# Zero stores of an output: some late in the filter stages, the others during the feed-forward

## The chip, the cores and the metric

One core of one Trainium2 chip runs the whole program. The metric is the device time of one execution in microseconds; lower is better. Before the change three runs took 1114.2 us (median), between 1113.84 and 1117.29.

## The reference, cut to what matters

```
X = rfft(x, axis=1); Y = X * (filt_r + i filt_i); x = irfft(Y)      # x: 8 batches, 3072 rows, 256 columns
x = x.reshape(24576, 256)
logits = x @ w_gate; expert = argmax(logits); gate = max softmax of the logits
for i in order: if counts[expert[i]] < 768: the row gets the next slot of its expert
y = relu(slots @ w1) @ w2                                            # 8 experts, 768 slots each
out = zeros(24576, 256); out[i] = gate[i] * y[slot of i] where i has a slot
out = elu(out @ w_in) @ w_out                                        # 256 -> 2048 -> 256
```

Only 6144 of the 24576 rows have a slot. A row without one is zero before the last product and so stays zero behind it: the output is 24 MB of zeros with 6144 rows written over them.

## The kernel before, in words

The program has two parts. The **filter stages** take the batches one by one. Three batches are taken at first (`run(3, True, "f")`); if these fill every expert, which a flag tells at the end, nothing else is done, and else all is done again with eight batches. In the profiled run the three are enough. Per batch `b` there are three generators: `p1` transforms over n1 in 8 steps of 4 rows (L195 and after), `p2` does the transform over n2, the filter and the transform back over k2 in 17 steps, and `p3` goes back to tokens in 18 steps and queues their rows for the slots. `route(b)` finds the slots, in small steps on VectorE. The loop of `run` weaves them: `p2(b)`, then the rest of `p1(b + 1)` with steps of `route(b)`, then `p3(b)` with the rest of `route(b)` and, in its last three steps, the first three of `p2(b + 1)`. The order of instructions on each engine is the order in which this Python code calls them (`manual_schedule`); engines wait for each other by semaphores.

GpSimd stores the rows to their slots in DRAM with indirect DMAs (`scatter`, L363), drawn from the queue `pq` by `pool_tick`. The second queue, `dq`, holds the **zero stores**: `zero_out(n)` writes the 1024 rows n of the output (1 MB) from a tile of zeros, with one DMA issued on ScalarE's queue (L432). `dma_tick` takes one from `dq`. Before the change `dq` gets all 24 behind the first `p1`, and is ticked on even steps below 12 of `p2(b)` for b > 0, on steps 4 to 7 of `p1(b + 1)`, and on every fourth step of `p3(b)` but for the last batch. Since the last three steps of `p3` take three of `p2`, the loop over `p2(1)` and `p2(2)` sees steps 3 to 16 and ticks at 4, 6, 8 and 10. That makes 4 + 5 + 4 + 4 + 5 ticks up to the end of `p3(1)`, and the last two stores go at steps 4 and 6 of `p2(2)`.

SP issues all loads: the rows of x (L187), the experts' weights (L516 and L520, `fetch`, called by `more_raw`), the rows of a chunk of slots (L538). Late in `p2(2)` it loads the first expert's weights; `load_piece` splits them (ScalarE's cast `wp`, L529, and a subtraction).

The **feed-forward** takes 16 chunks of 384 slots. `e1` does an expert's two products on a chunk (`ph` and `py`, in 8 blocks of hidden units), `e2` the shared two (`ph2`, then `po`, in 16 blocks). `do_e2` runs five chunks behind `do_e1`. In `e2` a block is six products into PSUM (three buffers), two activations on ScalarE (L632, L633), one operation on VectorE that reads PSUM for the last time (L634), a cast and a subtraction for the split in two parts, and six products into `po`, which run three blocks late. Behind the last block three indirect DMAs on GpSimd write 384 rows to their places in the output (L666). They wait for the zero stores before them, since both write the output; among themselves they are declared free of order (group `g_out`).

Of the kernel before, what the change touches and what calls it, by code (L numbers as in the profile page):

```python
# [25 lines left out]

# columns of the packed constant table
C_ID, C_WA, C_WD, C_TRI, C_ONE, C_KEY, C_RST, C_TOK = 0, 128, 224, 320, 416, 512, 520, 776
# [3 lines left out]
def shape_tables():  # L32
    """Transform matrices and index tables; they depend on the shapes alone.

    s = 32 n1 + n2 and f = k1 + 96 k2: a transform over n1, one over n2 per unit k1 = 1..47 with
    the twiddle in it, and unit 0 for the two real rows k1 = 0 and k1 = 48. The frequencies above
    S / 2 are kept as the conjugates of those below.
    """
    wa, wd = np.zeros((N1, 96)), np.zeros((96, N1))
# [52 lines left out]
class Moe:  # L92
# [23 lines left out]

    # ---------------------------------------------------------------- constants
    def consts(self, pool):
# [29 lines left out]
    def warm_up(self):  # L148
        """Keeps the tensor engine's clock up until the first rows are there."""
        ps = self.ps.tile([128, 128], F32, tag="pl", name="pwarm")  # L150
        z = self.zero[:, :128]
        for _ in range(10):
            self.nc.tensor.matmul(ps, lhsT=z, rhs=z, start=True, stop=True)

    # ---------------------------------------------------------------- filter tables
    def load_filters(self, g):
        """A third of the filter's rows and of the transforms over n2 and k2."""
        nc = self.nc
        big = self.big
        if g == 0:  # L160
            self.frt, self.fit, self.wbt, self.wct = [], [], [], []
        wb = big.tile([128, 8, 128], F32, tag="B", name="wbt", bufs=NBUF)
        nc.sync.dma_start(wb, self.wb[:, 8 * g : 8 * g + 8])
        for i in range(2):
            js = slice(8 * g + 4 * i, 8 * g + 4 * i + 4)
            fi = big.tile([128, 4, D], F32, tag="B", name="fit", bufs=NBUF)
            nc.sync.dma_start(fi[0:64], self.fi[0:64, js])
            fr = big.tile([128, 4, D], F32, tag="B", name="frt", bufs=NBUF)
            nc.sync.dma_start(fr, self.fr[:, js])
            self.fit.append(fi)  # L170
            self.frt.append(fr)
        wc = big.tile([128, 8, 128], F32, tag="B", name="wct", bufs=NBUF)
        nc.sync.dma_start(wc, self.wc[:, 8 * g : 8 * g + 8])
        self.wbt.append(wb)
        self.wct.append(wc)
# [6 lines left out]

    # ---------------------------------------------------------------- spectral filter of a batch
    def load_x(self, b, t):
# [9 lines left out]
    def p1(self, b):  # L194
        """The transform over n1: zt[d, m, n2]."""  # L195
        nc = self.nc
        self.zt = [self.big.tile([128, 96, N2], F32, tag="Z", name="zt", bufs=2) for h in range(2)]
        for t in range(8):
            xt = self.xq.popleft()
            for h in range(2):  # L200
                ps = self.ps.tile([128, 4, 96], F32, tag="pa" if h else "pb", name="pz")
                for i in range(4):
                    nc.tensor.matmul(ps[:, i], lhsT=xt[:, i, h * 128 : h * 128 + 128], rhs=self.wa, start=True, stop=True)  # L203
                dst = self.zt[h][:, :, 4 * t : 4 * t + 4]
                src = ps.rearrange("p n m -> p m n")
                if h:
                    nc.vector.tensor_copy(dst, src)
                else:
                    nc.scalar.copy(dst, src)
            if b:  # L210
                self.more_x()
            yield t

    def p2(self, b):
        """Per four rows m: the transform over n2, the filter, and the transform over k2."""
        nc = self.nc
# [55 lines left out]
    def route(self, b):  # L272
        """Logits, gates and slots of a batch's tokens, in steps that yield."""
        nc = self.nc
# [76 lines left out]
        if b >= self.spec_b:  # L351
            # The first chunks are read before this batch's rows are stored: it leaves them alone.
            low = late.tile([N1, N2], F32, name="low")
            nc.vector.tensor_scalar(low, pos, float(CH), BIG, op0=ALU.is_le, op1=ALU.mult)
            nc.vector.tensor_tensor(km, km, low, op=ALU.add)
# [20 lines left out]
    def store(self, b, t, y, rt):  # L376
        """Queues the four rows a partition has in y for their slots."""
        dst, gid = rt
# [9 lines left out]
    def p3(self, b):  # L388
        """Back over m to tokens, and their rows to the slots."""
        nc = self.nc  # L390
# [37 lines left out]

    # ---------------------------------------------------------------- slots and output
    def zero_out(self, n):  # L430
        o = self.out[n * 1024 : n * 1024 + 1024].rearrange("(p r) d -> p r d", p=128)
        self.nc.scalar.dma_start(o, self.zero.unsqueeze(1).to_broadcast([128, 8, D]))  # L432

    def prefill(self):
        """Every slot starts as a row of zeros with a token out of bounds."""
        nc = self.nc
# [6 lines left out]

    # ---------------------------------------------------------------- shared weights
    def slot(self, dtype, name):
# [7 lines left out]
    def convert(self):  # L453
        """Takes the shared weights, float64 words, into two float32r parts each, in steps that yield.

        P = sign 2^(e - 31); the high part takes the first 12 bits of the mantissa, the low part
        is rounded from the 20 bits after them.
        """
        nc = self.nc
# [48 lines left out]

    # ---------------------------------------------------------------- experts' weights
    def fetch(self, e, g):  # L510
        """Loads the weights of two of an expert's blocks of hidden units."""
        nc = self.nc
# [10 lines left out]
    def load_piece(self, first=False):  # L523
        """Splits the weights of the next block of hidden units in two parts."""
        nc = self.nc
# [6 lines left out]

    # ---------------------------------------------------------------- feed-forward
    def load_rows(self, c):
# [9 lines left out]
    def prep_x(self, c):  # L544
        """A chunk's rows times their gates, turned and split, in steps that yield."""
        nc = self.nc
# [32 lines left out]
    def e1(self, c, pieces, xh, xl):  # L579
        """An expert's two products on a chunk, per block of hidden units."""  # L580
        nc = self.nc
# [36 lines left out]
    def e2(self, yt, ids, tags, eng):  # L618
        """The shared products on a chunk, per block of hidden units, and its rows out."""
        nc = self.nc  # L620
# [26 lines left out]
        def down(f, rows=range(3)):  # L647
# [4 lines left out]
            for t in rows:  # L652
# [9 lines left out]
                if f == 15:  # L662
# [7 lines left out]
                        in_offset=None,  # L670
                        bounds_check=NB * S - 1,
                        oob_is_err=False,
# [21 lines left out]
    def ffn(self):  # L694
# [50 lines left out]
        def do_e2(c, nxt):  # L745
# [4 lines left out]
            for f in range(16):  # L750
                up(f)
                flush(3)
                lag.append(lambda *rows, f=f: down(f, *rows))
                next(conv, 0)
                if nxt < n and f in (5, 8, 11):
                    if f == 5:
                        prep = self.prep_x(nxt)
                    next(prep, 0)
                    if f == 11:
                        more_rows()  # L760
# [12 lines left out]

    # ---------------------------------------------------------------- the whole
    def run(self, nb, spec, tagname):
# [5 lines left out]
        with ExitStack() as st:  # L781
# [22 lines left out]
            self.prefill()  # L804
            self.dq.extend((lambda n=n: self.zero_out(n)) for n in range(24))
            p2 = self.p2(0)
            self.ffn_open()
            for b in range(nb):
# [3 lines left out]
                for s in p2:  # L812
                    self.pool_tick()
                    if b and s % 2 == 0 and s < 12:
                        self.dma_tick()
# [9 lines left out]
                for t in p1:  # L825
                    next(rt, 0)
                    self.pool_tick(2)
                    if t > 3:
                        self.dma_tick()
# [14 lines left out]
                for s in p3:  # L844
# [4 lines left out]
                    self.pool_tick()  # L849
                    if s % 4 == 0 and not last:  # L850
                        self.dma_tick()
# [18 lines left out]
            for _ in prep:  # L870
                pass
            self.dma_tick(99)
            self.pool_tick(99)
            while len(self.pieces.get(0, [])) < 8:
# [18 lines left out]
def tile_fftconv_moe_elu(ctx, tc, x, fr, fi, wg, w1, w2, w_in, w_out, tab, wb, wc, disp, out, cap):  # L893
    k = Moe(tc, x, fr, fi, wg, w1, w2, w_in, w_out, tab, wb, wc, disp, out, cap)
    nc = tc.nc
    with tc.manual_schedule():
        if cap != 2 * CH:
            k.run(NB, False, "g")
            return
        # Three batches fill every expert, or else all of it is done again with all batches.  # L900
        flag = ctx.enter_context(tc.tile_pool(name="flag", bufs=1))
# [47 lines left out]
```

## Time and profile before

| | us |
|---|---|
| median of 3 runs | 1114.2 |
| lowest, highest | 1113.84, 1117.29 |
| profiled execution, span from its first to its last instruction | 1174.5 |
| TensorE busy in that span | 1067.7 |
| VectorE, ScalarE, GpSimd busy | 655.6, 670.5, 259.6 |

The page gives no other time for the profiled execution than its span; it is 60 us over the median of the runs without a profile. The page's rows by slices of the span show TensorE nearly always busy from about 450 us on and less before; the DMA engines are busy nearly all of the first 100 us, half until 250 us and little later.

### The profile page before, as it was taken

To read this page: it belongs to the slowest core of one execution; us is meant where nothing else is said; L and a number is where in the kernel's file an instruction comes from. 1 tells how busy PE (TensorE), PEld (TensorE's weight loads), DVE (VectorE), ACT (ScalarE), POOL (GpSimd) and SP (SyncE) were. 2 spreads that over 40 slices of the span, in tenths; PEclk is the share of its full clock that TensorE was granted. 3 is DMA by queue.
4 is the path that set the end of the run, shared out by engine and by line. 5 is a ranking of instruction groups with operands and counts; after the bars stand their busy time and mean duration, and the time that the engine had idled before them with its cause. 6 is when DMAs were issued, how large, how long until landed. Compare 5 with 4: busy or idle time off the path is not lost.

```text
span 1174.5 us, 17246 instructions
## 1 busy us (share of the span) xinstructions
PE 1067.7 (91%) x6164; PEld 982.3 (84%) x6164; DVE 655.6 (56%) x1222; ACT 670.5 (57%) x1411; POOL 259.6 (22%) x271
## 2 busy tenths in 40 slices
PE   7968789686298999999999999999999999999996
PEld 7857666564287888999999999999999999999996
DVE  1825645485169898754564455456555544555553
ACT  2625335365055547674675657467675746666664
POOL 0301570485626455400010010001101000111110
PEclk8978898798599999999999999999999999999998
DMA  9999558532245341300120030012211000000000
GB/s 251 267 211 320 177 171 275 175 102 68 69 142 169 97 146 54 91 23 14 33 68 28 1 99 15 15 32 68 63 55 33 1 15 1 14 15 14 15 15 16
DMA packets 86383, 100.89 MB, mean 86 GB/s; under 512 B 7404, under 2 KB 72385, under 8 KB 86288
## 3 DMA queue, kind: packets, MB, share of 16 engines
q1 hardware_dynamic: 54416, 61.88, 19.3%
q10 hardware_dynamic: 24960, 25.17, 6.4%
q0 software_dynamic: 6912, 12.65, 3.3%
q8 instruction: 50, 0.82, 0.3%
q14 instruction: 45, 0.37, 0.1%
HBM read 55.52 MB, written 47.31 MB: 88 GB/s over the span
## 4 chain that ended last, share of the span: by engine, by line
PE 70%; DVE 12%; issue 7%; DMA 4%; ACT 2%; POOL 2%; ACTq 1%; another core or an unknown queue 1%; SPq 0%; POOLq 0%; DVEq 0%
PE po L654 13%; PE ph L575 10%; PE ph L576 10%; PE ph L577 10%; PE po L661 7%; PE pz L203 3%; PE py L575 3%; PE py L577 3%; PE py L576 3%; DMA xt<-in_x_dram 2%; PE pv L399 2%; DVE hl L597 1%; PE pd L410 1%; PE pd L412 1%; DMA fit<-in_fi_dram 1%
## 5 line engine op out<-in xcount | busy, mean ns | idle before, releaser
L634 DVE SCALAR_TENSOR_TENSOR g<-g,ph 128x384 f32<-128x384 f32 x256 | 141.6, 553 | 237.5 <-ACT g L633 231.7
L654 PE MATMUL po<-wz,gh 128*128 128x512 f32 x576 | 210.2, 395 | 0.0
L632 ACT ACTIVATE g<-ph 128x384 f32<-128x384 f32 x256 | 125.5, 490 | 128.8 <-PE ph L577 128.3
L666 POOL DMA_INDIRECT out_dram<-o,ids x48 | 48.3, 1006 | 636.0 <-DVE o L665 625.0
L575 PE MATMUL ph<-y,wih 128*128 128x384 f32 x512 | 175.8, 343 | 1.7 <-DVE hl L597 1.0
L576 PE MATMUL ph<-y,wih 128*128 128x384 f32 x512 | 173.4, 339 | 0.0
L577 PE MATMUL ph<-y,wil 128*128 128x384 f32 x512 | 172.8, 338 | 0.0
L661 PE MATMUL po<-wz,gl 128*128 128x256 f32 x576 | 161.3, 280 | 0.0
L633 ACT ACTIVATE g<-g 128x384 f32<-128x384 f32 x256 | 134.6, 526 | 8.1
L644 DVE TENSOR_TENSOR gl<-g,gh 128x384 fp32r<-128x384 f32 x240 | 132.3, 551 | 3.7 <-ACT gh L643 3.7
L643 ACT CAST gh<-g 128x384 fp32r<-128x384 f32 x256 | 127.5, 498 | 5.2 <-PE po L654 4.0
L654 PEld LDWEIGHTS po<-wz,gh 128*128 128x128 f32 x576 | 108.1, 188 | 16.7
L597 DVE SCALAR_TENSOR_TENSOR hl<-ph,hh 128x384 fp32r<-128x384 f32 x128 | 71.0, 555 | 83.9 <-ACT hh L596 82.6
L596 ACT ACTIVATE hh<-ph 128x384 fp32r<-128x384 f32 x128 | 62.0, 489 | 87.6 <-PE ph L577 71.7
L661 PEld LDWEIGHTS po<-wz,gl 128*128 128x128 f32 x576 | 108.6, 189 | 0.0
L575 PEld LDWEIGHTS ph<-y,wih 128*128 128x128 f32 x512 | 96.1, 188 | 11.6 <-DVE g L634 2.1
L363 POOL DMA_INDIRECT disp_dram<-yr,dst x96 | 91.5, 953 | 50.8 <-issue 22.3
L577 PEld LDWEIGHTS ph<-y,wil 128*128 128x128 f32 x512 | 96.2, 188 | 0.0
L576 PEld LDWEIGHTS ph<-y,wih 128*128 128x128 f32 x512 | 96.2, 188 | 0.0
L575 PE MATMUL ph<-xh,wp 128*128 128x384 f32 x256 | 90.3, 353 | 4.4 <-DVE hl L597 3.8
L575 PE MATMUL py<-hh,wp 128*128 128x384 f32 x256 | 87.0, 340 | 3.4 <-ACT hh L596 3.4
L576 PE MATMUL py<-hl,wp 128*128 128x384 f32 x256 | 87.4, 342 | 2.3 <-DVE hl L597 2.0
(129 smaller groups left out, 2015.6 us busy)
## 6 DMA issues: line engine op xcount, KB each, us to landing
out_dram<-zero ACTq DMA_DIRECT2D x24, 1024.0 KB
raw<-in_w_dram SPq DMA_DIRECT2D x88, 128.0 KB
raw<-in_w_dram SPq DMA_DIRECT2D x44, 256.0 KB
xt<-in_x_dram SPq DMA_DIRECT2D x24, 384.0 KB
disp_dram<-prow SPq DMA_DIRECT2D x16, 387.0 KB
xr<-disp_dram SPq DMA_DIRECT2D x16, 387.0 KB
r<-in_w_in_dram SPq DMA_DIRECT2D x8, 512.0 KB
r<-in_w_out_dram SPq DMA_DIRECT2D x8, 512.0 KB
```

The lines of the kernel that those rows point to most:

```text
L363: r = self.nc.gpsimd.indirect_dma_start(out=self.disp, out_offset=bass.IndirectOffsetOnAxis(ap=dst[:, n : n + 1], axis=0), in_=y[:, i, :], ...
L575: mm(ps, lhsT=wh, rhs=xh, start=first, stop=False)
L576: mm(ps, lhsT=wh, rhs=xl, start=False, stop=False)
L577: mm(ps, lhsT=wl, rhs=xh, start=False, stop=last)
L597: nc.vector.scalar_tensor_tensor(hl, ps, 0.0, hh.bitcast(F32), op0=ALU.max, op1=ALU.subtract)
L632: nc.scalar.activation(g, ps, AF.Relu, scale=-1.0)
L633: nc.scalar.activation(g, g, AF.Exp, scale=-1.0)
L634: nc.vector.scalar_tensor_tensor(g, g, -1.0, ps, op0=ALU.add, op1=ALU.max)
L643: nc.scalar.copy(gh, g)
L644: eng.tensor_tensor(gl, g, gh.bitcast(F32), op=ALU.subtract)
L654: nc.tensor.matmul(po[t].rearrange("p a d -> p (a d)"), lhsT=gh[:, c], rhs=wo.rearrange("p a d -> p (a d)"), start=(f == 0), stop=False,)
L661: nc.tensor.matmul(po[t][:, 1], lhsT=gl[:, c], rhs=wo[:, 0], start=False, stop=(f == 15))
```

## The change

Of the 24 zero stores the first nine (the rows of the three batches in use) are queued in the filter stages, and the ticks there are made fewer: with three batches in use, none in `p1`, none in `p3(0)` and `p2(1)`, so that five go in `p3(1)` and four in `p2(2)`. The other 15 (rows of batches not in use, which no slot's token can name) are queued behind the loop and ticked in blocks 2 and 10 of each `e2`. These 15 are declared free of order with the scatters to the output, and the scatter's bound is lowered to the rows of the batches in use. Some comments are emptied; the line count ahead of the changed code stays the same.

```diff
     def zero_out(self, n):
         o = self.out[n * 1024 : n * 1024 + 1024].rearrange("(p r) d -> p r d", p=128)
-        self.nc.scalar.dma_start(o, self.zero.unsqueeze(1).to_broadcast([128, 8, D]))
+        r = self.nc.scalar.dma_start(o, self.zero.unsqueeze(1).to_broadcast([128, 8, D]))
+        if n >= self.nb * S // 1024:
+            self.tc.declare_no_dep(r.ins, group=self.g_out, reason="no token of these batches has a slot")
+            self.tc.add_to_no_dep_group(self.g_out, r.ins)
...
-                        bounds_check=NB * S - 1,
+                        bounds_check=self.nb * S - 1,
...
                 lag.append(lambda *rows, f=f: down(f, *rows))
                 next(conv, 0)
+                if f in (2, 10):
+                    self.dma_tick()
...
-            self.dq.extend((lambda n=n: self.zero_out(n)) for n in range(24))
+            low = nb * S // 1024
+            self.dq.extend((lambda n=n: self.zero_out(n)) for n in range(low))
...
-                    if b and s % 2 == 0 and s < 12:
+                    if b and s % 2 == 0 and s < 12 and (not spec or b > 1):
                         self.dma_tick()
...
-                    if t > 3:
+                    if t > 3 and not spec:
                         self.dma_tick()
...
-                    if s % 4 == 0 and not last:
+                    if s % 4 == 0 and not last and (not spec or b):
                         self.dma_tick()
...
             self.dma_tick(99)
+            self.dq.extend((lambda n=n: self.zero_out(n)) for n in range(low, NB * S // 1024))
             self.pool_tick(99)
```

## Rows read from the trace of the kernel before

**Rows 1.** The page's first line.
```profile
span 1174.5 us, 17246 instructions
```
**Rows 2.** Windows: stretch, its length, busy us (instructions) per engine, clock, DMA share, rate.
```profile
90.00:95.00 5.00, 5.00 (x45) 4.92 (x45) 2.61 (x6) 1.75 (x4) 0.00 (x0) 1.00 0.90 279
100.00:105.00 5.00, 3.37 (x12) 2.03 (x10) 2.47 (x7) 2.62 (x5) 0.19 (x1) 0.50 1.06 371
...
200.00:250.00 50.00, 39.76 (x229) 32.88 (x228) 32.62 (x52) 23.66 (x46) 28.14 (x31) 0.86 0.53 169
500.00:600.00 100.00, 100.00 (x575) 95.73 (x574) 51.69 (x102) 64.31 (x139) 5.99 (x6) 1.00 0.10 33
```
**Rows 3.** Chain of waits, in order of time: start us, us, what.
```profile
94.70 2.66 ACTq L432
97.98 3.77 ACTq L432
...
186.48 2.49 ACTq L432
189.59 2.82 ACTq L432
```
**Rows 4.** All zero stores by their line: shortest, median, longest in ns.
```profile
L432 ACTq DMA_DIRECT2D out_dram<-zero x24: 541/542/4325, 89.2 to 235.0; - x24
```
**Rows 5.** Timeline of ScalarE, first place: start us, us, what.
```profile
94.23 3.13 ACTq L432 DMA_DIRECT2D out_dram<-zero  x1
...
97.43 4.33 ACTq L432 DMA_DIRECT2D out_dram<-zero  x1
...
106.55 0.54 ACTq L432 DMA_DIRECT2D out_dram<-zero  x1
...
111.14 0.54 ACTq L432 DMA_DIRECT2D out_dram<-zero  x1
```
**Rows 6.** Timeline of VectorE, both places; in brackets idle time before, and releaser.
```profile
98.02 0.69 DVE L403 TENSOR_TENSOR vl<-pv,vh 96x512 fp32r<-96x512 f32 x1 [1.11 <-ACT vh L402]
...
102.46 0.69 DVE L403 TENSOR_TENSOR vl<-pv,vh 96x512 fp32r<-96x512 f32 x1 [3.39 <-ACT vh L402]
...
189.62 0.69 DVE L403 TENSOR_TENSOR vl<-pv,vh 96x512 fp32r<-96x512 f32 x1 [0.93 <-ACT vh L402]
...
193.12 0.69 DVE L403 TENSOR_TENSOR vl<-pv,vh 96x512 fp32r<-96x512 f32 x1 [2.44 <-ACT vh L402]
```
**Rows 7.** Timeline of TensorE, both places: the products `pd`.
```profile
102.48 0.74 PE L410 MATMUL pd<-vh,wdh 96*96 96x512 f32 x1 [1.63 <-ACT vh L402]
...
106.78 0.47 PE L410 MATMUL pd<-vh,wdh 96*96 96x512 f32 x1
...
107.90 0.47 PE L410 MATMUL pd<-vh,wdh 96*96 96x512 f32 x1
...
193.14 0.74 PE L410 MATMUL pd<-vh,wdh 96*96 96x512 f32 x1 [1.17 <-ACT vh L402]
...
199.29 0.48 PE L410 MATMUL pd<-vh,wdh 96*96 96x512 f32 x1
```
**Rows 8.** Timeline of ScalarE, stage `p2(2)`.
```profile
228.20 0.54 ACTq L432 DMA_DIRECT2D out_dram<-zero  x1
...
235.00 0.54 ACTq L432 DMA_DIRECT2D out_dram<-zero  x1
...
256.96 1.14 ACT L529 CAST wp<-raw 128x512 fp32r<-128x512 f32 x2
```
**Rows 9.** Waits of SP's queue: us in total, times, longest us.
```profile
SPq L516 <- DMA out_dram<-zero: 17.6, 2, 15.3
```
**Rows 10.** Waits of ScalarE between 480 and 1100 us.
```profile
ACT g L632 <- PE ph L577: 110.6, 161, 2.7
```
**Rows 11.** Timelines of VectorE and TensorE in an `e2`.
```profile
607.56 0.55 DVE L634 SCALAR_TENSOR_TENSOR g<-g,ph 128x384 f32<-128x384 f32 x1 [0.33 <-ACT g L633]
...
610.97 0.34 PE L575 MATMUL ph<-y,wih 128*128 128x384 f32 x1
```

## The prediction

> **What bounds the kernel now.** I read first the page's header, then the windows, then the chain of waits, and only then the timeline around the stores that the change moves. The span of the profiled execution is 1174.5 us [rows 1]. The windows split the span in two unlike halves [rows 2]: in the feed-forward TensorE is busy for 100.00 of 100 us at a granted clock of 1.00 while the DMA engines are 10% used, so nothing that stays beside TensorE there costs time; in the filter stages it is busy for 39.76 of 50 us at 0.86, with the DMA engines 53% used; there it waits for its feeders, and the chain of waits passes through ScalarE, VectorE and the DMAs. A change in the first half moves the end by what it takes out of that chain; in the second half it costs nothing unless TensorE is made to wait.
>
> The chain contains four pieces that belong to the zero stores themselves: issuing stores on ScalarE's queue at 94.70, 97.98, 186.48 and 189.59, for 2.66 + 3.77 + 2.49 + 2.82 = 11.74 us [rows 3]. They lie in two places that are the same place of the program, the change from the transform over n1 of the next batch to `p3`: four stores come from the last four steps of `p1`, a fifth from step 0 of `p3`. Of the 24 issues the median takes 542 ns, the longest 4325 ns [rows 4]. The long ones are the fourth and fifth of each burst: 3.13 and 4.33 us [rows 5]. Where a store follows 4.59 us behind the last one, it takes 0.54 us (106.55 and 111.14) [rows 5]. So the issue is short when the stores are spaced and long when five come at once; ScalarE, which has the casts of `p3` behind them in its queue, stands still meanwhile.
>
> **The change part by part.**
>
> *First batch boundary: four stores of `p1(1)`, five of `p3(0)` and four of `p2(1)` go.* Both long issues of this place go. What is late next is read from VectorE, which waits for ScalarE's cast `vh`: it was idle 1.11 us before the first residual `vl` and 3.39 us before the second [rows 6], because between them it has the small operations of `route`. So not all of the chain's 6.43 us can be had: VectorE's own work takes their place, and I take its idle time, 4.50 us.
>
> *Second batch boundary: the four stores of `p1(2)` go; the one of `p3(1)` step 0 stays, now alone.* By rows 5 a store alone issues in 0.54 us and ScalarE goes on behind it. VectorE's idle time here is 0.93 + 2.44 = 3.37 us [rows 6], against 5.31 us in the chain.
>
> *The clock behind both places.* TensorE had a granted clock of 1.00 (its 2.4 GHz level) at 90 to 95 us, and 0.50 (1.2 GHz) at 100 to 105 us, behind the idle time that the held casts made [rows 2]. The products `pd` start 4.30 us apart over two steps there (102.48 to 106.78), and 1.12 us apart once the clock is back (106.78 to 107.90) [rows 7]: 4.30 - 2.24 = 2.06 us lost. At the second place three steps take 6.15 us (193.14 to 199.29), 6.15 - 3.36 = 2.79 us lost. Together 4.85 us, if the clock stays up once the holds are gone. Some idle time between cast, residual and product stays, so the ends are 0 and 4.85; I take the middle, 2.4 us.
>
> *Nine stores instead of 24 in the filter stages.* `p3(1)` ticks at steps 0, 4, 8, 12 and 16, `p2(2)` at 4, 6, 8 and 10: exactly nine, so none is left for the flush behind the loop. Seven of them issue where seven did before; the old list ran out behind the two at 228.20 and 235.00 [rows 8], so those at steps 8 and 10 are new there. At that spacing of 6.80 us each is a short issue. The 15 issues fewer are worth between 0 and 15 x 0.54 = 8.1 us; I take 0, since of all issues only the four long ones are pieces worth naming in the chain [rows 3].
>
> *SP's weight loads.* They do wait for zero stores, though they share no buffer: 17.6 us in two waits, the longest 15.3 us [rows 9]. Since the late nine now stand directly ahead of these loads, this wait moves onto the loads for the first expert. What is queued behind them on SP is the load of the first rows; who waits is ScalarE's cast `wp` of the third pair of blocks, at 256.96 [rows 8]. With a store each 6.80 us after 235.00, the last but one issues at 241.8. With 4.6 us for it (the spacing at which ScalarE was not held, rows 5) and as much again for the load behind it, the load has landed at 251.0, some 6 us before the cast: I take 0. The upper end is the first rival's.
>
> *Fifteen stores in the feed-forward,* at blocks 2 and 10 of each of the first eight `e2`. Each is 0.54 us on ScalarE. Behind it stands the activation of block 3, whose result VectorE has read from PSUM at 607.56 + 0.55 = 608.11; TensorE overwrites such a buffer three blocks later, at 610.97 [rows 11]. That is 2.86 us of cover for 0.54 us, and at block 10 ScalarE waits for TensorE anyway (110.6 us in 161 waits between 480 and 1100 us [rows 10]). With the cover gone it would be 8.1 us. The DMA engines are 10% busy there [rows 2]; the group that frees the stores from the scatters means POOL's scatters wait for none of them. Cost 0.
>
> *The bound check* changes a constant; the scatter's instruction stays what it was. The nine early stores, which the output scatters do wait for, are issued in the filter stages; the first such scatter comes behind the last block of the first `e2`.
>
> Here the Trainium skill can be weighed against the rows. Its page DMA: Bandwidth & Descriptors, section Issuing engines are not separate DMA queues, says that transfers from all issuing engines share the same 16 DMA engines, and that the sequencer's time to start one is usually small beside the transfer. By that rule moving 15 issues moves bandwidth alone and the sum would be near 0. The median issue agrees with it; the four long issues of rows 3 and 5 do not, and it is on them that the sum rests.
>
> **Sum.** 4.50 + 3.37 + 2.4 + 0 + 0 + 0 = 10.3 us, to be taken from the profiled execution: 1174.5 - 10.3 = 1164 us of span. The lower end is 0, since nothing is added at the two places and the stores moved away are covered; the upper is 11.74 of the chain plus 4.85 of the clock, 16.6 us, and a little of the 8.1 on top. The runs have a median of 1114.2 us, 60 us under that span; the page does not say where the 60 us lie. The two holds come from the order of the issues and from 1 MB per store, so I take the same microseconds off the median: 1114.2 - 10.3 = 1103.9, say 1104.
>
> **Rivals.**
> *1. Half is given back at the weights.* A load behind the store at 241.8 that waits as long as the longest wait did, 15.3 us, issues at 257.1; with 4.6 us to land (the spacing at which a whole store was absorbed) it is 4.7 us late for the cast at 256.96. For it: the wait exists in the trace. Against it: 15.3 us came behind a burst of five, which is gone. Time 1108.7, about 1109.
> *2. Nothing comes of it.* The holds are of the profiled execution, whose span is 60 us above the median, or the loads of x that run at the same time hold the same steps. For it: the DMA engines are 90 to 106% used in the windows around the first place [rows 2]. Against it: VectorE's idle time names ScalarE's cast, and the chain names the issues. Time 1114. The rule of the Trainium skill above would give this time too.
> *3. Slower: ScalarE is held in the feed-forward.* If each of the 15 stores takes the 4.33 us of the longest issue, 4.33 - 2.86 = 1.47 us reach TensorE each time, 22 us in all, and the time is 1104 + 22 = 1126. It decides from 10.3 / 15 = 0.69 us per store on, an issue of 3.5 us. Against it: the long issues come only in bursts, and here a store follows eight blocks behind the last, on DMA engines that are 10% busy.
> That the change does not do what it says would be a tenth store left over or a scatter that waits for the late ones; the count above and the shared group exclude both.
>
> **How the numbers follow.** Forecast 0.66, rival 1 0.17, rival 2 0.10, rival 3 0.07. A measurement of this kernel can tell about 0.3%, 3.3 us, from no change: faster is under 1110.9, slower over 1117.5. Faster: nearly all of the forecast and most of rival 1, 0.79; same: most of rival 2 and the edge of rival 1, 0.13; slower: rival 3 and an unlucky end of rival 2, 0.08. The range goes from 1096 (17 us and a little of the hidden issues) to 1114 (rival 2); outside lie rival 3, half of rival 2 and some 0.04 below.
>
> **What would show it.** After the change no issue of a zero store over about 1 us; no pieces of them in the chain; VectorE's idle time before the first two residuals of each `p3` under 1 us; granted clock not at 0.50 behind `p1`; 15 short issues, two in each of the first eight `e2` but the last, with TensorE still at 100%; the first `ph` of the feed-forward some 10 us sooner. Wrong it would be if long issues appear in `p3(1)` or in `e2`, if `wp` waits for its load, or if the time won at the boundaries shows up as idle time before the feed-forward.

## The result, and the profile after

The changed kernel takes 1105.1 us (median of 4 runs, 1102.43 to 1105.83), the kernel before, run beside it, 1115.2 us (1113.84 to 1117.29): a ratio of 0.990 with a 95% interval of 0.988 to 0.992, 10.1 us less. The forecast was 1104.0. All four runs of the changed kernel had a mean granted clock of 0.979 to 0.982; of the 24 runs of four kernels told below in which no issue is over 1.6 us, 11 had 0.975 to 0.982 and took 1105.2 to 1107.7 us, and 13 had 0.971 to 0.975 and took 1109.4 to 1111.4, so part of the 10.1 us may be the draw of these four.

The profile of [rows 1] cannot be subtracted from the one after: on one chip the kernel before takes 1172 us in the median of 27 runs, with a span of 1171.3 us in its profile there, on the other chips 1114 to 1118, and I take [rows 1] to come from such a slower chip. For it: in the trace of [rows 1] ScalarE has 37.4 us of waits whose end the profile puts down to none of the core's engines or DMAs (it calls them `remote`); the four profiles from the chip with 1172 us have such waits too, the others have none. What they are is not shown. So the kernel before was profiled once more on a chip where it takes 1118.0 us (the first experiment below); that profiled execution took 1118.09 us, the one of the changed kernel 1104.82. Their first lines, before and then after:

```profile
span 1116.0 us, 17246 instructions
```
```profile
span 1102.9 us, 17247 instructions
```

All zero stores by their line (shortest, median and longest issue in ns), the kernel before in its second profile:

```profile
L432 ACTq DMA_DIRECT2D out_dram<-zero x24: 541/542/4580, 89.0 to 206.0; - x24
```

and the changed kernel, with the time from issue to landing:

```profile
L432 ACTq DMA_DIRECT2D out_dram<-zero x24: 541/542/637, 162.1 to 739.6; - x24
...
DMA to landing us min/median/max: 4.7/5.1/9.2
```

No issue is long any more. The first place, on ScalarE's timeline: in the kernel before the fourth and fifth store of the burst hold ScalarE, and its casts `vh` come late (idle time and releaser in brackets, as everywhere below),

```profile
89.02 0.64 ACTq L432 DMA_DIRECT2D out_dram<-zero  x1
90.04 0.55 ACTq L432 DMA_DIRECT2D out_dram<-zero  x1
92.39 0.54 ACTq L432 DMA_DIRECT2D out_dram<-zero  x1
...
94.02 3.05 ACTq L432 DMA_DIRECT2D out_dram<-zero  x1
97.11 0.58 ACT L402 CAST vh<-pv 96x512 fp32r<-96x512 f32 x1 [2.62 <-PE pv L399]
97.14 4.58 ACTq L432 DMA_DIRECT2D out_dram<-zero  x1
101.81 1.07 ACT L402 CAST vh<-pv 96x512 fp32r<-96x512 f32 x2 [4.12 <-issue]
...
103.25 0.60 ACT L402 CAST vh<-pv 96x512 fp32r<-96x512 f32 x1
```

in the changed kernel the first three casts follow each other at once, and the fourth comes 3.64 us behind the first, where it came 6.14 us behind it before:

```profile
93.65 1.56 ACT L402 CAST vh<-pv 96x512 fp32r<-96x512 f32 x3 [0.85 <-PE pv L399]
97.29 0.58 ACT L402 CAST vh<-pv 96x512 fp32r<-96x512 f32 x1 [0.33 <-PE pv L399]
```

The second residual `vl` on VectorE, for which [rows 6] has 3.39 us of idle time, has 3.65 in the second profile of before,

```profile
102.42 0.69 DVE L403 TENSOR_TENSOR vl<-pv,vh 96x512 fp32r<-96x512 f32 x1 [3.65 <-ACT vh L402]
```

and none in the changed kernel, at either place:

```profile
94.93 0.66 DVE L403 TENSOR_TENSOR vl<-pv,vh 96x512 fp32r<-96x512 f32 x1
95.87 0.68 DVE L403 TENSOR_TENSOR vl<-pv,vh 96x512 fp32r<-96x512 f32 x1
...
163.33 0.66 DVE L403 TENSOR_TENSOR vl<-pv,vh 96x512 fp32r<-96x512 f32 x1
164.27 0.68 DVE L403 TENSOR_TENSOR vl<-pv,vh 96x512 fp32r<-96x512 f32 x1
```

Windows (columns as in [rows 2]: TensorE first, the granted clock third from the end), before:

```profile
100.00:105.00 5.00, 3.14 (x11) 1.81 (x10) 2.51 (x7) 2.62 (x5) 0.19 (x1) 0.50 1.06 370
105.00:110.00 5.00, 5.00 (x18) 3.66 (x18) 2.79 (x6) 2.84 (x5) 0.00 (x0) 0.53 1.09 385
```

and after, where the clock stays at its upper level and the feed-forward, now with stores in it, keeps TensorE busy throughout (its DMA share is 0.24, that of [rows 2] 0.10):

```profile
100.00:105.00 5.00, 5.00 (x34) 4.00 (x33) 4.03 (x11) 4.70 (x10) 1.16 (x2) 1.00 0.00 0
105.00:110.00 5.00, 5.00 (x33) 3.91 (x32) 3.15 (x5) 4.76 (x10) 3.81 (x5) 1.00 0.29 83
...
500.00:600.00 100.00, 100.00 (x575) 95.86 (x574) 51.44 (x102) 63.46 (x137) 5.99 (x6) 1.00 0.24 79
```

The span splits by program marks: `p3` has 16 casts `vh`, so the first and sixteenth of each `p3` are the same points in every variant, and the first `ph` begins the feed-forward. Worked out from the rows of these casts, in us; the last three columns are experiments told below:

| stage | before, second profile | after | before - after | first burst alone | second burst alone | 24 spaced |
|---|---|---|---|---|---|---|
| start to first cast of `p3(0)` | 97.11 | 93.65 | 3.46 | 96.31 | 94.01 | 99.23 |
| `p3(0)`, first to last cast | 22.68 | 17.16 | 5.52 | 21.45 | 17.18 | 16.73 |
| to first cast of `p3(1)` | 53.37 | 51.24 | 2.13 | 51.22 | 53.99 | 51.23 |
| `p3(1)`, first to last cast | 19.80 | 17.16 | 2.64 | 17.17 | 19.94 | 17.18 |
| to first cast of `p3(2)` | 36.07 | 36.08 | 0.0 | 36.03 | 36.07 | 36.10 |
| `p3(2)`, first to last cast | 27.16 | 25.55 | 1.6 | 27.22 | 27.22 | 24.06 |
| to first `ph` | 2.8 | 3.7 | -0.9 | 3.7 | 3.7 | 2.8 |
| first `ph` to the end | 857.0 | 858.3 | -1.3 | 857.5 | 857.0 | 860.3 |

The sum of the differences is 13.1 us, that of the spans. 10.3 of it lie in the three rows from `p3(0)` to the end of `p3(1)`, where the two bursts were.

### The profile page after: what moved, and what is told of

It is laid out like the page before. It is cut to its first block, busy times and chain, and to the rows that moved or that the text cites. A ratio compares the mean times of both kernels' runs of the same rounds, so it can differ in the third digit from the quotient of the medians.

```text
span 1102.9 us, 17247 instructions
## 1 busy us (share of the span) xinstructions
PE 1045.3 (95%) x6164; PEld 970.9 (88%) x6164; DVE 657.5 (60%) x1222; ACT 670.1 (61%) x1411; POOL 259.7 (24%) x271
## 3 DMA queue, kind: packets, MB, share of 16 engines
q10 hardware_dynamic: 24960, 25.17, 6.8%
## 4 chain that ended last, share of the span: by engine, by line
PE 75%; DVE 12%; DMA 4%; issue 3%; POOL 2%; ACT 2%; SPq 1%; POOLq 0%; ACTq 0%; DVEq 0%
PE po L657 15%; PE ph L578 11%; PE ph L579 11%; PE ph L580 11%; PE po L664 8%; PE pz L203 3%; PE py L579 3%; PE py L580 3%; PE py L578 3%; DMA xt<-in_x_dram 2%; PE pv L399 1%; DVE hl L600 1%; DVE uu L249 1%; DMA fit<-in_fi_dram 1%; DVE cp L503 1%
## 5 line engine op out<-in xcount | busy, mean ns | idle before, releaser
L657 PEld LDWEIGHTS po<-wz,gh 128*128 128x128 f32 x576 | 108.1, 188 | 16.7
```

The source lines that it names most:

```text
L657: nc.tensor.matmul(po[t].rearrange("p a d -> p (a d)"), lhsT=gh[:, c], rhs=wo.rearrange("p a d -> p (a d)"), start=(f == 0), stop=False,)
```

## Experiments

Each was timed beside the kernel before on the same chip; "gain" is 1 less the ratio, times the time of before, with its 95% interval.

**The kernel before once more.** No edit.

> The kernel before, unchanged, profiled once more. Its first profiled execution has a span of 1174.5 us against a median of 1115.2, the changed kernel's 1102.9 against 1105.1. If the 1174.5 was an execution disturbed as a whole: a span near 1113, feed-forward from about 255 us on, and the long issues of zero stores still there at the same two places (sum of the four 9 to 13 us). If it is the way this kernel is always profiled: 1170 again. If the long issues themselves belonged to the disturbed execution: none over 1 us.

> The kernel before, unchanged, for a profile of it whose time lies near the median of its runs (1115 to 1117 us). My theory: the two bursts still hold ScalarE, the fourth and fifth issue of each for 2 to 4.5 us, at both batch boundaries, and TensorE's granted clock falls to 0.50 behind the first. The rival, that the holds belong to the profiled execution with the span of 1174.5 us: all 24 issues under 1 us, as in the other executions of this kernel that ran in 1172 us only the second place had two over 1 us.

The first ran on the chip with 1172 us and took 1173.27 us: the 27 runs beside it, without a profile, were as long, so it is not the profiler that makes such a span. It shows what lets a burst pass:

```profile
83.96 0.63 ACTq L432 DMA_DIRECT2D out_dram<-zero  x1
...
93.24 0.54 ACTq L432 DMA_DIRECT2D out_dram<-zero  x1
95.80 0.54 ACTq L432 DMA_DIRECT2D out_dram<-zero  x1
```

In this execution the steps of `p1` came slower, the five stores took 11.84 us to come, and none was held. At the second place of this execution they took 7.63 us, and the fourth and fifth were held for 1.84 and 3.33 us. In the second execution, shown above, the fourth came 5.00 us behind the first and was held for 3.05 us. The second execution (1118.09 us) has holds of 3.05 and 4.58 us at the first place and of 1.82, 3.17 and 2.99 at the second, where the third store is held too: the holds belong to the kernel at its usual time as well, and the rival that they were the slow profile's own falls.

**Fewer pieces, same bytes, same places.** The kernel before, with each store made of 512 runs of 2 KB in place of 1024 of 1 KB (an earlier temporary of `route` is reused to make room for the wider tile of zeros):

```diff
-        self.zero = pool.tile([128, D], F32, name="zero")
+        self.zero = pool.tile([128, 2 * D], F32, name="zero")
...
-            low = late.tile([N1, N2], F32, name="low")
+            low = mx
...
-        o = self.out[n * 1024 : n * 1024 + 1024].rearrange("(p r) d -> p r d", p=128)
-        self.nc.scalar.dma_start(o, self.zero.unsqueeze(1).to_broadcast([128, 8, D]))
+        o = self.out[n * 1024 : n * 1024 + 1024].rearrange("(p a r) d -> p a (r d)", p=128, r=2)
+        self.nc.scalar.dma_start(o, self.zero.unsqueeze(1).to_broadcast([128, 4, 2 * D]))
```

> The kernel before, its 24 stores where they were, but each written from a tile of zeros with two rows per partition: 512 pieces of 2 KB in place of 1024 of 1 KB. If the issue is held by the number of pieces still queued: five stores are 2560 pieces, fewer than the three that passed without a hold: no issue over 1 us, 1105 to 1109. If it is held by the bytes still queued: long issues as before, 1113 to 1117.

Measured: 1106.8 us beside 1117.4 of before, ratio 0.992 (0.990 to 0.994), a gain of 8.9 us (6.4 to 11.4). Its timeline of ScalarE, first place:

```profile
86.97 0.64 ACTq L432 DMA_DIRECT2D out_dram<-zero  x1
87.84 0.67 ACTq L432 DMA_DIRECT2D out_dram<-zero  x1
90.19 0.54 ACTq L432 DMA_DIRECT2D out_dram<-zero  x1
91.82 0.54 ACTq L432 DMA_DIRECT2D out_dram<-zero  x1
93.14 0.58 ACT L402 CAST vh<-pv 96x512 fp32r<-96x512 f32 x1 [0.85 <-PE pv L399]
93.15 1.57 ACTq L432 DMA_DIRECT2D out_dram<-zero  x1
```

and its window behind the place:

```profile
95.00:100.00 5.00, 4.86 (x34) 4.00 (x35) 4.63 (x15) 4.45 (x9) 0.19 (x1) 1.00 1.03 393
```

The five stores come as close together as in the kernel before, the DMA engines are as full (1.03, 393 GB/s), and yet the fourth issue is short, the fifth takes 1.57 us in place of 4.58, and the clock stays at 1.00. Expected by the number of pieces was no issue over 1 us; two are over it, this one and the fifth at the second place (1.59 us). How much was queued when the fourth store was issued can be worked out from the packets of ScalarE's queue (q10) that had started by then: number, MB and share, in the second profile of before and in this run,

```profile
q10 hardware_dynamic: 1233, 1.25, 26.2%
```
```profile
q10 hardware_dynamic: 672, 1.34, 30.4%
```

Of the 3.15 MB of the first three stores 1.9 MB were still to go before and 1.8 MB here; at the fifth store, in the same way, 2.5 MB and 2.6 MB. So the bytes under way were the same and the hold was not: it goes by the pieces far more than by the bytes. Their number alone does not give it either: here the fifth store was held behind some 1240 pieces, and in the kernel before the third was not held behind some 1380. Shortening the holds gives nearly all of the gain with every store where it was.

That is also the answer to the rule that the prediction weighed: the Trainium skill, page DMA: Bandwidth & Descriptors, section Issuing engines are not separate DMA queues, calls the sequencer's time usually small beside the transfer. That holds for the 542 ns of the median issue and not for the 4.58 us of the fifth, where a store lands 7.1 us (median) after its issue. The same page of the Trainium skill, section Why a DMA increments its semaphore by 16 and not by 1, says that one descriptor moves one contiguous run of the last dimension. By it halving the runs halves the descriptors, and the trace agrees: q10 has 24960 packets in the kernel before and 12672 here.

**All 24 spaced in the filter stages.** The kernel before, without the stores in `p1`, and with those of `p2` on every even step:

```diff
-                    if b and s % 2 == 0 and s < 12:
+                    if b and s % 2 == 0:
                         self.dma_tick()
...
-                    if t > 3:
-                        self.dma_tick()
```

> The kernel before with all 24 zero stores still in the filter stages, but none in p1: they go on even steps of p2(1) and p2(2) up to 16 and every fourth step of p3(0) and p3(1), so never five at once. Theory (the gain is ScalarE no longer held by the fourth and fifth store of a burst): no issue over about 1 us, 1105 to 1107 us, as fast as the changed kernel. Rival (the gain is 15 MB less for the DMA engines in the filter stages): 1113 to 1116, as the kernel before.

> All 24 zero stores stay in the filter stages, none in the transform over n1, spaced over p3 and p2. If the holds are the whole cost and the place of the stores does not matter: about 1106 us where before takes 1116, ratio 0.991, no issue over 1 us. If the volume of 24 MB in the filter stages costs the time: 1116 us, ratio 1.000.

On the chip with 1172 us the ratio was 0.996 (0.993 to 0.998), a gain of 4.9 us (1.9 to 8.1), about half of what was expected, and why is not shown; on a chip with 1118.0 us the kernel took 1110.2, ratio 0.992 (0.991 to 0.994), a gain of 8.5 us (6.3 to 10.6), with no issue over 0.64 us. Moving the 24 MB out of the filter stages is not what pays: left there and spaced, they give the gain too on the second chip, within the intervals. That is against the rival of the bandwidth.

**One burst put back.** The changed kernel with its nine early stores as the burst at the first batch boundary (four in `p1(1)`, five in `p3(0)`), and in a second kernel at the second boundary (`b == 1` for `b == 0`):

```diff
-                    if b and s % 2 == 0 and s < 12 and (not spec or b > 1):
+                    if b and s % 2 == 0 and s < 12 and not spec:
                         self.dma_tick()
...
-                    if t > 3 and not spec:
+                    if t > 3 and (not spec or b == 0):
                         self.dma_tick()
...
-                    if s % 4 == 0 and not last and (not spec or b):
+                    if s % 4 == 0 and not last and (not spec or b == 0):
                         self.dma_tick()
```

> The changed kernel with its nine early stores moved back to the first place: four in p1(1), five in p3(0), none later; 15 in the feed-forward as they are. Theory: two long issues at the first place come back, 4.5 us of VectorE's idle time and half of 2.1 us for the clock: 1110 to 1111. Rival (bandwidth, or the weights' loads behind the late stores): 1102 to 1105.

> The changed kernel with its nine early stores at the second place: four in p1(2), five in p3(1), none in p2(2). Theory: two long issues there, 3.4 us of VectorE's idle time and half of 2.8 us for the clock: 1109 to 1110; with e2 the two losses add up to the whole gain of 10.1. Rival (bandwidth): 1103 to 1106.

> The changed kernel with its nine early stores put back as the burst at the first batch boundary. By the prediction's terms the change then keeps the second place alone, 3.37 + 1.4 (half of 2.79) = 4.8 us: 1111 us where before takes 1116, ratio 0.9957. If only the first place ever cost time: 1116 us, ratio 1.000.

> The changed kernel with its nine early stores put back as the burst at the second batch boundary. By the prediction's terms the change then keeps the first place alone, 4.50 + 1.03 (half of 2.06) = 5.5 us: 1110.5 us where before takes 1116, ratio 0.995. If only the second place ever cost time: 1116 us, ratio 1.000; if the burst is short here for want of stores still under way from the first place: 1106 us, ratio 0.991.

On the chip with 1118.0 us: first burst alone 1112.3 us, ratio 0.9955 (0.9939 to 0.9971), a gain of 5.0 us (3.2 to 6.8) for taking the second away; second burst alone 1112.8, ratio 0.9966 (0.9950 to 0.9981), 3.8 us (2.1 to 5.6) for taking the first away. Expected were 4.8 and 5.5. Both lie in the intervals, the second barely. Within them each burst costs its part whether the other is there or not: 5.0 + 3.8 = 8.8 us together, against 8.5 for the spaced kernel and 10.1 for the change. The table shows the burst where it was put: `p3(0)` takes 21.45 us with the first and 17.18 without; the way to `p3(1)` and `p3(1)` itself take 53.99 + 19.94 with the second, 51.22 + 17.17 without, 5.5 us more. With the second burst alone, its third and fourth issue, the first cast of `p3(1)`, and the fifth issue:

```profile
159.47 2.53 ACTq L432 DMA_DIRECT2D out_dram<-zero  x1
162.07 3.07 ACTq L432 DMA_DIRECT2D out_dram<-zero  x1
165.18 0.58 ACT L402 CAST vh<-pv 96x512 fp32r<-96x512 f32 x1 [2.65 <-issue]
165.50 2.64 ACTq L432 DMA_DIRECT2D out_dram<-zero  x1
```

On the chip with 1172 us the same two gave ratios of 0.998 (0.996 to 1.000) and 0.9945 (0.9925 to 0.9964). There the first burst held ScalarE for 3.54 and 4.20 us, and the second passed without a hold (longest issue 0.63 us) in the profiled execution: its five stores took 11.84 us to come there. Taking the second burst away gains 1.9 us (-0.5 to 4.2) on this chip, less than the 4.8 expected, and taking the first away 6.4 (4.2 to 8.8).

**No late stores, and none at all.** The changed kernel without the 15 stores of the feed-forward (the rows of the five batches not in use are then not written), and without any of the 24 (no row without a slot is written):

```diff
-            self.dq.extend((lambda n=n: self.zero_out(n)) for n in range(low))
...
-            self.dq.extend((lambda n=n: self.zero_out(n)) for n in range(low, NB * S // 1024))
```

The first kernel takes out only the lower line.

> The changed kernel without its 15 stores in the feed-forward (these rows of the output are not written): what they cost there. Theory (2.86 us of cover for 0.54 us each): 1104 to 1106, no change against the changed kernel. Rival (ScalarE held, or the weights' loads slowed): up to 8 us faster, 1097 to 1102.

> The changed kernel without any zero store (rows without a slot are not written): what the nine late ones still cost. Theory: spaced stores cost nothing, 1103 to 1106. Rival (the nine slow the first weights or the scatters): 1096 to 1102.

Measured beside 1117.4 us of before: 1108.0 us, ratio 0.991 (0.989 to 0.994), and 1109.6 us, ratio 0.992 (0.991 to 0.994). Neither is faster than the change, 0.990 (0.988 to 0.992), though the changed kernel was not run again on this chip. So the 15 stores in the feed-forward and the nine ahead of the weights cost nothing that can be measured within intervals of some 2 us, and no placing of zero stores can be seen to win more than the change did.

**The 15 as a burst in the feed-forward.** The changed kernel with one store in each block of one `e2`:

```diff
-                if f in (2, 10):
+                if nxt == self.AHEAD + 3:
                     self.dma_tick()
```

> The changed kernel with its 15 late stores one per block in a single e2 (the third), 2.1 us apart where the DMA engines took one per 3 to 4.4 us in the burst before. Theory: from the fourth on each issue takes over 1 us, ScalarE falls behind, TensorE's cover of some 3 us is used up and it waits: 12 blocks x 0.9 to 2.3 us less 3 us of cover, 8 to 25 us slower than the changed kernel, 1113 to 1130. Rival (in the feed-forward an issue is hidden whatever it takes): 1104 to 1106.

Measured: 1116.1 us, ratio 0.999 (0.997 to 1.001): the whole gain is gone again. On ScalarE, first four stores short, then held:

```profile
478.41 0.56 ACTq L432 DMA_DIRECT2D out_dram<-zero  x1
...
484.25 0.54 ACTq L432 DMA_DIRECT2D out_dram<-zero  x1
485.83 1.47 ACTq L432 DMA_DIRECT2D out_dram<-zero  x1
487.93 2.38 ACTq L432 DMA_DIRECT2D out_dram<-zero  x1
...
504.09 4.06 ACTq L432 DMA_DIRECT2D out_dram<-zero  x1
...
518.03 2.05 ACTq L432 DMA_DIRECT2D out_dram<-zero  x1
```

and TensorE, which was at 100.00 of 100 us, is at 95.81:

```profile
500.00:600.00 100.00, 95.81 (x530) 90.33 (x530) 49.61 (x97) 59.82 (x130) 5.99 (x6) 0.98 0.38 126
```

From the first `ph` (243.9 us) to the end of the span (1111.2) it takes 867.3 us, against 858.3 in the changed kernel. The third rival's mechanism is real; what keeps it from the change is the spacing alone, one store every eight blocks.

## Why the prediction was right, point by point

*The holds.* Right in the cause and in the sum; how the sum divides between the holds and the clock came out otherwise. The late stores of a burst hold ScalarE (the fourth and fifth, and at the second place the third too, 1.82 us, and 1.07 us in the prediction's own trace), the long issues are gone (longest 0.64 us), and on the chips at 1114 to 1118 us the change and every experiment that takes the holds away or shortens them at both places gain 8.5 to 10.1 us, wherever the stores go. The terms were 4.50 + 1.03 us for the first place and 3.37 + 1.40 for the second, the clock's half included. The stages between the casts give 5.52 and 2.13 + 2.64 = 4.77, the runs 3.8 (2.1 to 5.6) and 5.0 (3.2 to 6.8). That the stages agree with the terms so closely is luck in two ways. VectorE's 1.11 us before its first residual [rows 6] belong to the hold ahead of the first cast, which the table counts in its first line. And the two parts of the sum are both off, in opposite directions. Each `p3` can be split at its fourth cast, before which the last long issue has ended. At the first place this cast comes 6.14 us behind the first before and 3.64 after; at the second place it stands in these rows, before and after, 4.55 and 3.64 us behind the first:

```profile
177.71 0.60 ACT L402 CAST vh<-pv 96x512 fp32r<-96x512 f32 x1
```
```profile
165.69 0.58 ACT L402 CAST vh<-pv 96x512 fp32r<-96x512 f32 x1 [0.33 <-PE pv L399]
```

So in the three stages the holds are worth 2.50 + 2.13 + 0.91 = 5.5 us, where the terms without the 1.11 us were 3.39 + 3.37 = 6.8. VectorE's 3.39 us overstate the first place: in the changed kernel, without any hold, the fourth cast also comes 3.64 us behind the first, so part of the hold covers time that passes anyway. The chain's price (11.74 us, [rows 3]) would have been too high, as argued.

*The clock.* Right in sign, too small in size: 1.00 behind `p1` at the first place, where it was 0.50 and 0.53. From the fourth to the sixteenth cast, with no long issue left, `p3(0)` takes 16.54 us before and 13.53 after, `p3(1)` 15.25 and 13.52. TensorE is what bounds this stretch before: it is busy for 5.00 of 5 us from 105 to 110 us with 18 matmuls at 0.53, where the changed kernel has 33 at 1.00, and from 175 to 180 us with 21 at 0.50. So some 3.0 + 1.7 = 4.7 us go with the clock, by one profile of each kernel. The prediction's two ends were 0 and 4.85; it took the middle because some idle time would stay, but the clock stayed up at both places, and the upper end is what came.

*Nine in place of 24, and the weights.* Worth nothing, as put: without any store the kernel is no faster. SP's waits for zero stores at the weights' loads did grow, as foreseen, from 22.5 us in three waits (and 2.9 in one at L520) in the second profile of before,

```profile
SPq L516 <- DMA out_dram<-zero: 22.5, 3, 15.3
```

to 27.7 us in four in the changed kernel ([rows 9] had 17.6 in two),

```profile
SPq L519 <- DMA out_dram<-zero: 27.7, 4, 15.8
SPq L523 <- DMA out_dram<-zero: 9.2, 2, 4.6
```

but the casts `wp` up to 250 us did not wait, and over the whole span they waited 0.6 us for a load (1.1 before). The last figure of this row, from the groups by line of the changed kernel between 95 and 250 us, is ScalarE's idle time before them:

```profile
L532 ACT CAST wp<-raw 128x512 fp32r<-128x512 f32 x10 | 6.1, 625 | 0.0
```

The first rival falls with it. A load of x's rows also waited for zero stores in the second profile of before (16.7 us, once) and no longer does. That is no part of the gain: the kernels with 2-KB runs and with 24 spaced stores have the gain and still wait there, 17.1 and 16.5 us.

*The 15 in the feed-forward.* Cost nothing, as put: 858.3 us from the first `ph` to the end, against 857.0 before and 857.5 without these stores. One thing did not come as announced: a piece of a zero store stands in the chain of waits of the changed kernel, once,

```profile
399.90 5.40 DMA out_dram<-zero
```

so something waited there for a landing. The run without these stores bounds its price by nothing that can be measured.

*The range's other reasons.* The first `ph` was to come 10 us sooner. It comes 14.4 us sooner than in the second profile of before (259.0 and 244.6), and 74.3 us sooner than in the one that the prediction was read from, 318.9. The doubt in the second rival, that the holds might be those of an execution 60 us too long, was right to raise and wrong in its outcome: the long issues are much the same in both profiles (3.13 and 4.33 us, 3.05 and 4.58), and the 60 us, all ahead of the first `ph` (318.9 against 259.0), came from elsewhere. One sign was put too widely: VectorE's idle time before the second residual was to be under 1 us in each `p3`, and in `p3(2)`, which has no zero store, it is 2.67 us before and after.

*What stays open.* The stage `p3(2)` holds no zero store, and still takes 27.2 us in the three profiles with a held burst before it, 25.6 after the change and 24.1 in the spaced kernel. In the second profile of before the clock is at 0.50 in one window of 5 us there; after the change none is under 0.77, and in the spaced kernel the mean from 200 to 250 us is 1.00. The stage's length goes with its mean granted clock in all nine profiles from the chips at 1114 to 1118 us: 27.2 us at 0.87 in the three with a held burst, 25.6 at 0.93 in four (the change, no late stores, the burst in `e2`, 2-KB runs), 24.1 at 1.00 in two (spaced, no stores). So the 1.6 us of this stage belong to the clock. Why it falls further behind a burst 50 us and more ahead, these profiles don't tell. Nor did a run change the clock alone.

## What to carry to other kernels

Issuing a DMA is cheap until several with many pieces are queued on one engine; then the engine that issues stands still with the compute behind it. Look in the timeline for issues far over the median, and space the transfers out, make their pieces longer, or queue them, spaced, in a stage where another engine sets the pace (as a burst there they cost the whole gain); which of the three is chosen mattered little here. Read the price from the engine that waits, not from the length of the issue, check how late the work behind it really comes (here the fourth cast, 2.5 us late behind an issue of 4.58), and look at the granted clock behind the place: here it was 4.7 of the 10.3 us in the three stages.

## What was not expected of the hardware

The hold goes by pieces far more than by bytes: of 1-MB stores in runs of 1 KB, the fourth, 5.00 us behind the first, is held 3.05 us and the fifth 4.58; in runs of 2 KB, with as many bytes queued, only the fifth, 1.57 us. In a longer burst (15 stores, of 478.41 to 518.03 us) one store goes each 2.83 us, 370 GB/s, while the DMA engines move 348 GB/s in all at a share of 1.05 (480 to 520 us): a held engine issues at about the rate at which they write.

The start of the same program differed by 6.75 us between two executions. The changed kernel and the one without the 15 late stores are identical up to the feed-forward; their first cast `vh` comes at 93.65 and at 100.40 us. In the latter, TensorE was granted its lower level until 100 us, in the former the upper from 90 on. The latter:

```profile
90.00:95.00 5.00, 5.00 (x23) 4.77 (x23) 1.40 (x3) 1.05 (x3) 0.00 (x0) 0.50 0.27 79
95.00:100.00 5.00, 5.00 (x26) 4.97 (x26) 1.75 (x4) 0.69 (x2) 0.00 (x0) 0.50 0.30 79
```

the former:

```profile
90.00:95.00 5.00, 4.75 (x42) 4.37 (x40) 3.60 (x9) 2.62 (x6) 0.00 (x0) 1.00 0.67 182
95.00:100.00 5.00, 4.36 (x29) 3.54 (x30) 4.84 (x15) 3.33 (x7) 0.19 (x1) 1.00 0.15 56
```

So how much of the 3.46 us in the table's first line is the hold ahead of the cast (ScalarE's 2.62 us of idle time in the second profile of before) can't be told, and a change of this size can't be read from two profiles alone.
